# Linear attention and two MLPs on one core: the row of maxima of q, turned and merged earlier, its two halves sent by two DMA queues

## The chip, the core and the metric

The kernel runs on one core of a Trainium2 chip. Its engines are TensorE (PE, with its weight loads PEld), VectorE (DVE), ScalarE (ACT), GpSimd (POOL) and SyncE (SP), which here only issues DMAs. Each engine works through its own stream of instructions in order and waits on semaphores of the others. The metric is the device time of one execution in microseconds (us).

## What is computed

Four batches of eight heads, 576 rows of 64 numbers; `w_phi` has 128 features. The attention's output, one row of 512 per token, goes through two MLPs of 2304 tokens, which take most of the time and which the change doesn't touch.

```python
def phi(x):
    proj = np.einsum('bhsd,df->bhsf', x, w_phi)
    proj = proj - np.max(np.abs(proj), axis=-1, keepdims=True)
    return np.concatenate([np.exp(proj), np.exp(-proj)], axis=-1)
q_p, k_p = (phi(q), phi(k))
kv = np.einsum('bhsf,bhsd->bhfd', k_p, v)
z = np.sum(k_p, axis=2)
num = np.einsum('bhsf,bhfd->bhsd', q_p, kv)
den = np.einsum('bhsf,bhf->bhs', q_p, z)[..., None] + 1e-06
...
h = (x @ w1) * (x @ w2) @ w3
x = h @ w_out
h = np.maximum(x @ w_in, 0.0)
out = (h * h) @ w_out2
```

The maximum of `abs(proj)` is subtracted, for q, inside a PSUM tile in which a token is a column; so the maxima of q have to become a row.

## The kernel before

The attention runs over 16 units, t = 0 to 15: a unit is a pair of heads of one batch. Even units also do the tails (the last 64 rows of a head) of k for themselves and the next unit (`project_k2`, `peak_k2`, `less_k2`, `exp_k2`); odd units turn the tails of the two units that follow. In the traces a unit carries its batch and pair: unit 5 is 1_1, unit 6 is 1_2.

The order of all instructions on all engines is written by hand. `START` (line 29) is the order of the first unit and of what goes ahead of it. `SLOT` (line 35) is the order of every later unit: names of steps, run from left to right; in one slot, steps of unit t stand among steps of the unit behind it (its output) and the unit ahead (its transposes). Each engine gets its instructions in this order and never out of it.

The steps of unit t on which the change bears, with the engine and the tile that the profile names:

- `project_q` (line 369, PE): q times `w_phi`, into the one PSUM tile `pq`. Since there is only one, the next unit's `project_q` waits until `exp_q1` has read it. Its start is taken here as the start of a unit.
- `max_q` (line 384, DVE, `m<-pq` L387): maxima over 32 rows, into `m1`.
- `max_rows` (line 392, PE, `pm` L395): a 128x128 transpose of `m1` into PSUM.
- `max_parts` (line 397, DVE): two reductions of `pm`, once into `m` in full precision (L400), once into `mh[:, 0]`, rounded for the matmul (L402), and their difference into `mh[:, 1]` (L403). Then two DMAs (L406), both by SP, write the high and the low part into rows 0 and 1 of the one tile `mrow`.
- `minus_q` (line 410, PE, `pq<-mrow` L414): a matmul with a matrix of -1, which subtracts both rows from `pq`.
- `exp_q0`, `exp_q1` (line 418, ACT, `qp` L421).
- `peak_k0`, `less_k0`, `exp_k0` (lines 343 to 367): `kmax` on DVE (L348), the difference `kp<-pk,kmax` on DVE (L358), two exponentials on ACT (L365); then the same for half 1.
- `turn_k`, `high_k`, `low_k` (lines 296 to 308): four transposes `pkt` of the next unit's k (PE L288), their rounded part `kT` (ACT L291), the rest (DVE L294). `turn_q`, `high_q`, `low_q` are the same for q, `pqt` and `qT`.
- `out`, `keep` (lines 454 and 486): `po` of the unit behind (PE L459), copied to `nd` (ACT L488).
- `w-1`, `w0`, `w1`: a step of decoding a weight. Two ACT instructions of it (L137, L112) come ahead of `high_k`; four DVE instructions (L114, L117, L121, L124) come between `low_q` and the next unit's `max_q`.

Of the kernel before, what the change touches and what calls it, by code (L numbers as in the profile page):

```python
# [10 lines left out]
F32R = mybir.dt.float32r  # L11
I32 = mybir.dt.int32
AF = mybir.ActivationFunctionType
ALU = mybir.AluOpType
AX = mybir.AxisListType
# [17 lines left out]
warm8/0 values0/0 turn_q/0 minus_q/0 high_q/0 exp_q0/0 low_q/0 values1/0 exp_q1/0  # L33
""".split()
SLOT = """
load_kq product_b project_q keep_values project_k0 turn_w3b split_w3b x_load max_q project_k1 w1 w1 w0 early turn_k peak_k0
max_rows high_k less_k0 max_parts w-1 late store_x exp_k0 out x_split0 x_split1 x_split2 feature_sums peak_k1 less_k1
keep turn_q low_k turn_tails project_k2 product_a0 exp_k1 denominators spread peak_k2 less_k2 high_q minus_q exp_k2
keep_tails exp_q0 values0 gate last turn_w3 x_split3 low_q w0 w0 exp_q1 w0 values1 keep_rest low_tail reciprocals split_w3
product_a1 quotients keep_a load_v tail_values  # L40
# [4 lines left out]
def attention_then_mlps(ctx: ExitStack, tc: tile.TileContext, q, k, v, w_phi, w1, w2, w3, wo, wi2, wo2, out):  # L45
    nc = tc.nc
# [157 lines left out]
    with ExitStack() as actx:  # L204
        att = actx.enter_context(tc.tile_pool(name="att", bufs=2, side="right"))
# [52 lines left out]
        nb = S // 32  # L258
# [137 lines left out]

        def max_parts(z):
            pm = z["pm"][0:2 * nb]
            m = att.tile([2 * nb, 32], F32, tag="m", name=f"m_{z['nm']}")
            nc.vector.tensor_reduce(m, pm.rearrange("p (a r) -> p r a", a=4), AX.X, ALU.max)  # L400
            mh = att.tile([2 * nb, 2, 32], F32R, tag="mh", name=f"mh_{z['nm']}")
            nc.vector.tensor_reduce(mh[:, 0], pm.rearrange("p (a r) -> p r a", a=4), AX.X, ALU.max)  # L402
            nc.vector.tensor_tensor(out=mh[:, 1], in0=m, in1=mh[:, 0].bitcast(F32), op=ALU.subtract)  # L403
            z["mrow"] = mrow
            for s in range(2):
                nc.sync.dma_start(  # L406
                    z["mrow"][s:s + 1].bitcast(F32).rearrange("s (k r) -> s k r", r=32), mh[:, s].bitcast(F32)
                )

# [136 lines left out]
        w2h, w3s_at, queue, loaded, halves = {}, {}, [], [], []  # L546
# [55 lines left out]
        def even(f, *at):  # L602
# [3 lines left out]
        steps = {  # L606
            "keep_values": (-1, keep_values),
            "project_q": (0, project_q), "max_q": (0, max_q), "max_rows": (0, max_rows), "max_parts": (0, max_parts),
            "minus_q": (0, minus_q), "exp_q0": (0, lambda z: exp_q(z, 0)), "exp_q1": (0, lambda z: exp_q(z, 1)),
            "turn_k": (1, turn_k), "high_k": (1, high_k), "low_k": (1, low_k),  # L610
# [82 lines left out]
        with tc.manual_schedule(engines=mine):  # L693
            for entry in START:
                name, t = entry.split("/")
# [11 lines left out]
    late = ctx.enter_context(tc.tile_pool(name="late", bufs=2, side="right", reuse_waits="tile"))  # L707
# [4 lines left out]
    def lunit(dtype, shape, name, tag="w", bufs=RIGHT):  # L712
        return late.tile([P] + shape, dtype, tag=tag, bufs=bufs, name=name)
# [207 lines left out]
    with tc.manual_schedule(engines=mine):  # L921
# [5 lines left out]
        for s, (grp, at, k) in enumerate(steps):  # L927
# [26 lines left out]
            else:  # L954
# [8 lines left out]
                if k == HG - 1:  # L963
# [7 lines left out]
                    out=g[:, 1, 0:n], in0=g32[:, 0:n], in1=g[:, 0, 0:n].bitcast(F32), op=ALU.subtract  # L971
# [45 lines left out]
        for at, (b, n) in enumerate(mlp2):  # L1017
            cs, nt = nxt, n // P
            ops = None
            for j in range(NR):  # L1020
# [15 lines left out]
                if last_step:  # L1036
# [5 lines left out]
                    out=r32[:, 0:n], in0=ph[:, 0:n], scalar=0.0, in1=t[:, 0:n], op0=ALU.max, op1=ALU.mult  # L1042
                )
                if last_step:
                    col_split(x_in[nb_], nn, f"y{at}_{nb_}", [2])
                r = lunit(F32R, [2, 512], f"r_{b}_{j}", "g", 3)
# [3 lines left out]
                    out=r[:, 1, 0:n], in0=r32[:, 0:n], in1=r[:, 0, 0:n].bitcast(F32), op=ALU.subtract  # L1050
# [46 lines left out]
```

## Time and profile before

| | us |
|---|---|
| median of 3 runs | 943.4 (942.83 to 944.54) |
| the profiled execution | 942.8 |
| its span, first to last instruction | 941.0 |
| PE, share of the span | 98% |
| DVE, ACT, POOL, share of the span | 58%, 41%, 27% |

The page gives busy time by engine over the whole span, and the span has two parts. Up to some 195 us the attention runs, with all engines in use; after that the MLPs keep PE busy with matmuls that follow one another without a gap. An average over both says little of the attention. There, what counts is which wait ends last in each unit, and for that the trace is read unit by unit.

### The profile page before, as it was taken

Reading aid. Unit: us, or ns where it says so; the run is one execution under the profiler, and the core shown is the slowest. Engines: PE = TensorE matmul, PEld = TensorE weight load, DVE = VectorE, ACT = ScalarE, POOL = GpSimd, SP = SyncE. Lnnn points to the kernel's source line nnn. Section 1 sums busy time; section 2 is a strip of 40 time slices with the busy share of each in tenths; the row PEclk is TensorE's granted clock in tenths of the full one; section 3 lists DMA queues with packets and bytes.
Section 4 is the critical chain, followed back from the end, with each engine's and each line's share of the span. In section 5 each row is a group of like instructions: output and inputs, shape, how many; then the busy total and the mean of one; then the engine's idle time right before and its main releaser. Section 6 shows DMA issues by size and latency. Waiting matters only on the chain.

```text
span 941.0 us, 14857 instructions
## 1 busy us (share of the span) xinstructions
PE 921.3 (98%) x5915; PEld 762.2 (81%) x5915; DVE 545.7 (58%) x892; ACT 382.6 (41%) x689; POOL 249.6 (27%) x304
## 2 busy tenths in 40 slices
PE   8899999999999999999999999999999999999997
PEld 7677777778888988888988888888888888888896
DVE  5899888878656456666856688852224223322332
ACT  4777777653322334432333344342223223222322
POOL 1566556554121123333423145520000000000000
PEclk9999999999999999999999999999999999999999
DMA  6565556345241334254443433211002000100000
GB/s 164 125 161 150 145 153 182 89 149 160 87 135 54 127 111 157 68 202 157 166 152 117 147 114 111 90 39 51 1 1 90 1 1 0 68 1 1 23 24 23
DMA packets 81110, 89.24 MB, mean 95 GB/s; under 512 B 44624, under 2 KB 65680, under 8 KB 81040
## 3 DMA queue, kind: packets, MB, share of 16 engines
q1 hardware_dynamic: 79712, 87.72, 29.9%
q8 instruction: 47, 0.77, 0.4%
q10 hardware_dynamic: 1328, 0.56, 0.3%
q14 instruction: 23, 0.19, 0.1%
HBM read 69.76 MB, written 18.35 MB: 94 GB/s over the span
## 4 chain that ended last, share of the span: by engine, by line
PE 89%; DVE 4%; ACT 3%; DMA 2%; issue 1%; SPq 0%; ACTq 0%
PE ph L183 21%; PE op L905 21%; PE yp L887 11%; PE pb L183 11%; PE pa L183 10%; PE pf L844 5%; PE po L459 2%; PE pk L250 2%; PE pq L380 2%; ACT qp L421 2%; PE pkv L432 2%; DMA mrow<-mh 1%; PE pd L481 1%; DVE kmax L348 1%; DVE m L387 1%; ACT kp L365 1%
## 5 line engine op out<-in xcount | busy, mean ns | idle before, releaser
L905 PE MATMUL op<-w_w,r 128*128 128x512 f32 x864 | 209.6, 390 | 0.1
L905 PEld LDWEIGHTS op<-w_w,r 128*128 128x128 f32 x864 | 161.1, 188 | 33.4 <-ACT r L1047 0.5
L183 PE MATMUL ph<-y,w_w 128*128 128x512 f32 (+1 forms) x768 | 163.9, 362 | 0.0
L1041 DVE SCALAR_TENSOR_TENSOR r<-ph,t 128x512 f32<-128x512 f32 (+1 forms) x80 | 51.1, 639 | 187.8 <-ACT t L1039 187.8
L183 PEld LDWEIGHTS ph<-y,w_w 128*128 128x128 f32 x768 | 133.3, 189 | 23.8
L1039 ACT ACTIVATE t<-ph 128x512 f32<-128x512 f32 (+1 forms) x80 | 44.5, 556 | 215.5 <-PE ph L183 215.5
L887 PE MATMUL yp<-g,w3o 128*128 128x512 f32 (+1 forms) x480 | 106.1, 370 | 0.0
L129 POOL TENSOR_TENSOR dt_w<-dt_w,dy_w 128x512 f32<-128x512 f32 x48 | 62.9, 1310 | 126.2 <-DVE dy_w L124 126.1
L887 PEld LDWEIGHTS yp<-g,w3o 128*128 128x128 f32 x480 | 83.7, 189 | 14.8
L183 PE MATMUL pa<-c,w_w12a 128*128 128x512 f32 (+1 forms) x432 | 93.6, 366 | 0.0
L183 PE MATMUL pb<-c,w_w12b 128*128 128x512 f32 (+1 forms) x432 | 93.6, 366 | 0.0
L183 PEld LDWEIGHTS pa<-c,w_w12a 128*128 128x128 f32 x432 | 75.1, 189 | 13.2
L183 PEld LDWEIGHTS pb<-c,w_w12b 128*128 128x128 f32 x432 | 75.2, 189 | 13.1
L1049 DVE TENSOR_TENSOR r<-r,r 128x512 fp32r<-128x512 f32 (+1 forms) x80 | 51.0, 638 | 41.2 <-ACT r L1047 37.5
L966 DVE TENSOR_TENSOR g<-pb,a 128x512 f32<-128x512 f32 (+1 forms) x39 | 24.8, 636 | 84.6 <-PE pb L183 80.0
L139 POOL TENSOR_TENSOR w_w<-dt_w,w_w 128x512 fp32r<-128x512 f32 x32 | 48.8, 1527 | 84.2 <-ACT w_w L137 84.2
L1047 ACT ACTIVATE r<-r 128x512 fp32r<-128x512 f32 (+1 forms) x80 | 47.2, 590 | 55.9 <-DVE r L1041 55.9
L506 POOL TENSOR_SCALAR rc<-dc 32x9 f32<-32x9 f32 x128 | 45.5, 356 | 57.8 <-DVE dc L496 50.7
L968 ACT ACTIVATE g<-g 128x512 fp32r<-128x512 f32 (+1 forms) x39 | 23.0, 589 | 91.7 <-DVE g L966 91.7
L958 ACT COPY a<-pa 128x512 f32<-128x512 f32 (+1 forms) x39 | 21.2, 543 | 81.2 <-PE pa L183 81.2
L365 ACT ACTIVATE kp<-kp 128x512 f32<-128x512 f32 (+1 forms) x80 | 46.9, 588 | 17.3 <-DVE kp L358 15.1
L121 DVE TENSOR_SCALAR dy_w<-dt_w 128x512 int32<-128x512 int32 x48 | 50.9, 1061 | 0.7
(135 smaller groups left out, 1282.0 us busy)
## 6 DMA issues: line engine op xcount, KB each, us to landing
x<-x_hbm SPq DMA_DIRECT2D x16, 512.0 KB
raw_w<-in_moe_w_dram SPq DMA_DIRECT2D x16, 512.0 KB
raw_w<-in_moe_w_in_dram SPq DMA_DIRECT2D x16, 512.0 KB
raw_w<-in_moe_w_out_dram SPq DMA_DIRECT2D x16, 512.0 KB
qm<-in_q_dram SPq DMA_DIRECT2D x32, 128.0 KB
km<-in_k_dram SPq DMA_DIRECT2D x16, 256.0 KB
vs<-in_v_dram SPq DMA_DIRECT2D x32, 128.0 KB
raw_wo<-in_moe_w_out_dram SPq DMA_DIRECT2D x8, 512.0 KB
```

Source lines behind the costliest of these rows:

```text
L121: nc.vector.tensor_scalar(out=e, in0=t, scalar1=-(1 << 23), scalar2=None, op0=ALU.bitwise_and)
L129: nc.gpsimd.tensor_tensor(out=w, in0=t.bitcast(F32), in1=e.bitcast(F32), op=ALU.add)
L139: nc.gpsimd.tensor_tensor(out=dst[:, 1], in0=w[0], in1=dst[:, 0].bitcast(F32), op=ALU.subtract)
L183: nc.tensor.matmul(ps[:, 0:n], a, c, start=kk + i == 0, stop=kk == KD - 1 and i == 2)
L365: nc.scalar.activation(z["kp", j][:, :, s, :], z["kp", j][:, :, 1, :], AF.Exp, scale=1.0 - 2.0 * s)
L506: nc.gpsimd.tensor_scalar(out=z["rc2"][i * 32:(i + 1) * 32, s, :], in0=z["dc"][at * 32:(at + 1) * 32, :], scalar1=1e-6, scalar2=None, op0= ...
L844: nc.tensor.matmul(pf, a, c, start=g + j + n == 0, stop=g == 1 and j == 3 and n == 2)
L887: nc.tensor.matmul(blk.yp[i][:, 0:blk.n], a, d, start=c % HG + s == 0, stop=c % HG == HG - 1 and s == 2)
L905: nc.tensor.matmul(ops[i], a, d, start=j + s == 0, stop=j == NR - 1 and s == 2)
L1041: nc.vector.scalar_tensor_tensor(out=r32[:, 0:n], in0=ph[:, 0:n], scalar=0.0, in1=t[:, 0:n], op0=ALU.max, op1=ALU.mult)
L1047: nc.scalar.activation(r[:, 0, 0:n], r32[:, 0:n], AF.Copy)
L1049: nc.vector.tensor_tensor(out=r[:, 1, 0:n], in0=r32[:, 0:n], in1=r[:, 0, 0:n].bitcast(F32), op=ALU.subtract)
```

## The change

In `SLOT`, `max_rows` goes ahead of `turn_k`, and `max_parts` ahead of `less_k0`. `START` is as it was. In `max_parts` the rounded reduction into `mh[:, 0]` now comes ahead of the one into `m`, and the DMA of the high row is issued by ACT (`nc.scalar`), that of the low row by SP. Sixteen DMA issues move from SP to ACT; no instruction is added or taken away.

```diff
-load_kq product_b project_q ... w1 w1 w0 early turn_k peak_k0
-max_rows high_k less_k0 max_parts w-1 late store_x exp_k0 out ...
+load_kq product_b project_q ... w1 w1 w0 early max_rows turn_k
+peak_k0 high_k max_parts less_k0 w-1 late store_x exp_k0 out ...
...
         def max_parts(z):
             pm = z["pm"][0:2 * nb]
+            view = pm.rearrange("p (a r) -> p r a", a=4)
+            mh = att.tile([2 * nb, 2, 32], F32R, tag="mh", name=f"mh_{z['nm']}")
+            nc.vector.tensor_reduce(mh[:, 0], view, AX.X, ALU.max)
             m = att.tile([2 * nb, 32], F32, tag="m", name=f"m_{z['nm']}")
-            nc.vector.tensor_reduce(m, pm.rearrange("p (a r) -> p r a", a=4), AX.X, ALU.max)
-            mh = att.tile([2 * nb, 2, 32], F32R, tag="mh", name=f"mh_{z['nm']}")
-            nc.vector.tensor_reduce(mh[:, 0], pm.rearrange("p (a r) -> p r a", a=4), AX.X, ALU.max)
+            nc.vector.tensor_reduce(m, view, AX.X, ALU.max)
             nc.vector.tensor_tensor(out=mh[:, 1], in0=m, in1=mh[:, 0].bitcast(F32), op=ALU.subtract)
             z["mrow"] = mrow
-            for s in range(2):
-                nc.sync.dma_start(
+            for s, queue in enumerate((nc.scalar, nc.sync)):
+                queue.dma_start(
                     z["mrow"][s:s + 1].bitcast(F32).rearrange("s (k r) -> s k r", r=32), mh[:, s].bitcast(F32)
                 )
```

On PE in unit 6, before (`pk` is the projection of k, `pkt` the turned k of unit 7, `pm` the turned maxima, `po` the output of unit 5):

```order
L250 MATMUL pk_1_2_0_1268<-wbd_132,kT_1_2_1113 128x256 x6
L250 MATMUL pk_1_2_1_1276<-wbd_132,kT_1_2_1113 128x256 x6
L288 MATMUL pkt_1_3_1288<-ident_73,km_1_3_1068 128x128 x4
L395 MATMUL pm_1_2_1295<-ident_73,m1_0_97 128x128
L459 MATMUL po_1_1_1312<-qp_1_1_1186,kv_1_1_1264 64x512 x4
```

The same place after the change:

```order
L250 MATMUL pk_1_2_0_1268<-wbd_132,kT_1_2_1113 128x256 x6
L250 MATMUL pk_1_2_1_1276<-wbd_132,kT_1_2_1113 128x256 x6
L395 MATMUL pm_1_2_1288<-ident_73,m1_0_97 128x128
L288 MATMUL pkt_1_3_1290<-ident_73,km_1_3_1068 128x128 x4
L460 MATMUL po_1_1_1312<-qp_1_1_1186,kv_1_1_1264 64x512 x4
```

`pm`, which needs `max_q`, now stands directly behind `pk`, with the four transposes of k behind it instead of ahead of it.

On DVE in unit 5, before:

```order
L387 TENSOR_REDUCE m1_1_98<-pq_1_1_1070 128x36
L348 TENSOR_REDUCE kmax_1_1_0_1109<-pk_1_1_0_1084 128x4
L358 TENSOR_TENSOR kp_1_1_0_1115<-pk_1_1_0_1084,kmax_1_1_0_1109 128x4x128
L400 TENSOR_REDUCE m_1_1_1117<-pm_1_1_1111 36x32
L402 TENSOR_REDUCE mh_1_1_1119<-pm_1_1_1111 36x32
L403 TENSOR_TENSOR mh_1_1_1119<-m_1_1_1117,mh_1_1_1119 36x32
L348 TENSOR_REDUCE kmax_1_1_1_1151<-pk_1_1_1_1092 128x4
```

After:

```order
L387 TENSOR_REDUCE m1_1_98<-pq_1_1_1070 128x36
L348 TENSOR_REDUCE kmax_1_1_0_1111<-pk_1_1_0_1084 128x4
L401 TENSOR_REDUCE mh_1_1_1115<-pm_1_1_1104 36x32
L403 TENSOR_REDUCE m_1_1_1117<-pm_1_1_1104 36x32
L404 TENSOR_TENSOR mh_1_1_1115<-m_1_1_1117,mh_1_1_1115 36x32
L358 TENSOR_TENSOR kp_1_1_0_1122<-pk_1_1_0_1084,kmax_1_1_0_1111 128x4x128
L348 TENSOR_REDUCE kmax_1_1_1_1151<-pk_1_1_1_1092 128x4
```

The three instructions of `max_parts` now stand ahead of the difference `kp`, for which ACT's exponentials wait.

On ACT in the same unit, before:

```order
L291 ACTIVATE kT_1_2_1113<-pkt_1_2_1104 128x512
L365 ACTIVATE kp_1_1_0_1115<-kp_1_1_0_1115 128x4x128 x2
L488 COPY nd_1_0_1155<-po_1_0_1129 128x512
L365 ACTIVATE kp_1_1_1_1153<-kp_1_1_1_1153 128x4x128 x2
L291 ACTIVATE qT_1_2_1179<-pqt_1_2_1157 128x512
L291 ACTIVATE tT_1_2_1184<-ptt_1_2_1163 128x256
L421 ACTIVATE qp_1_1_1186<-pq_1_1_1070 128x1152 x2
```

After:

```order
L291 ACTIVATE kT_1_2_1113<-pkt_1_2_1106 128x512
L407 DMA mrow_99<-mh_1_1_1115 1x36x32
L365 ACTIVATE kp_1_1_0_1122<-kp_1_1_0_1122 128x4x128 x2
L489 COPY nd_1_0_1155<-po_1_0_1129 128x512
L365 ACTIVATE kp_1_1_1_1153<-kp_1_1_1_1153 128x4x128 x2
L291 ACTIVATE qT_1_2_1179<-pqt_1_2_1157 128x512
L291 ACTIVATE tT_1_2_1184<-ptt_1_2_1163 128x256
L422 ACTIVATE qp_1_1_1186<-pq_1_1_1070 128x1152 x2
```

The issue of the high row stands between `kT` and the first exponentials of k, and everything that ACT does for the unit is queued behind it.

## Rows read from the trace of the kernel before

**Rows 1.** Windows, core 0: length, busy PE PEld DVE ACT POOL, clock, DMA share, GB/s.

```profile
55.77:67.27 11.50, 10.82 (x151) 8.33 (x149) 10.79 (x22) 8.76 (x17) 7.09 (x13) 1.00 0.53 145
67.27:77.76 10.49, 10.49 (x148) 8.13 (x149) 8.89 (x17) 8.50 (x16) 6.82 (x12) 1.00 0.59 145
89.25:100.81 11.56, 10.61 (x149) 8.13 (x147) 9.92 (x20) 8.63 (x16) 7.79 (x13) 1.00 0.60 162
122.80:134.72 11.92, 10.73 (x152) 8.32 (x150) 11.19 (x23) 8.92 (x16) 7.52 (x14) 1.00 0.58 153
156.75:168.33 11.58, 10.60 (x147) 8.13 (x147) 9.94 (x20) 8.52 (x16) 7.83 (x13) 1.00 0.78 231
205.00:941.00 736.00, 730.23 (x3470) 613.53 (x3469) 376.36 (x574) 237.25 (x429) 139.21 (x104) 1.00 0.24 80
```

**Rows 2.** Waits of PE, 20 to 181 us: total us, times, longest.

```profile
PE pq L414 <- DMA mrow<-mh: 5.8, 6, 1.3
```

**Rows 3.** Timeline, unit 7: start, us, engine, line, operation [idle before, releaser].

```profile
93.64 1.69 SPq L406 DMA_DIRECT2D mrow<-mh  x2
...
97.66 0.76 PE L414 MATMUL pq<-mrow,minus 128*128 128x512 f32 x3 [0.95 <-DMA mrow<-mh]
```

**Rows 4.** Chain that ended last, unit 7: start, us, what.

```profile
94.55 2.97 DMA mrow<-mh
```

**Rows 5.** Timeline of DVE, units 5 and 6.

```profile
70.55 0.69 DVE L358 TENSOR_TENSOR kp<-pk,kmax 128x512 f32<-128x512 f32 x1
71.16 0.27 DVE L400 TENSOR_REDUCE m<-pm 36x32 f32<-36x128 f32 x1
...
75.17 0.69 DVE L294 TENSOR_TENSOR qT<-pqt,qT 128x512 fp32r<-128x512 f32 x1 [0.70 <-ACT qT L291]
...
79.36 1.34 DVE L387 TRANSPOSE_TENSOR_REDUCE m<-pq 128x36 f32<-128x1152 f32 x1
```

**Rows 6.** Timeline of ACT, unit 5.

```profile
70.60 0.60 ACT L291 ACTIVATE kT<-pkt 128x512 fp32r<-128x512 f32 x1 [0.81 <-PE pkt L288]
71.28 1.29 ACT L365 ACTIVATE kp<-kp 128x512 f32<-128x512 f32 x2
72.59 0.59 ACT L488 COPY nd<-po 128x512 f32<-128x512 f32 x1
73.21 1.30 ACT L365 ACTIVATE kp<-kp 128x512 f32<-128x512 f32 x2
74.54 0.60 ACT L291 ACTIVATE qT<-pqt 128x512 fp32r<-128x512 f32 x1
75.03 0.38 ACT L291 ACTIVATE tT<-ptt 128x256 fp32r<-128x256 f32 x1
75.40 2.15 ACT L421 ACTIVATE qp<-pq 128x1152 f32<-128x1152 f32 x2
```

**Rows 7.** Timeline of PE, unit 6.

```profile
80.45 0.60 PE L288 MATMUL pkt<-ident,km 128*128 128x128 f32 x4
80.89 0.27 PE L395 MATMUL pm<-ident,m 128*128 128x128 f32 x1
```

**Rows 8.** Timeline of DVE and PEld, unit 1.

```profile
23.48 1.38 DVE L387 TRANSPOSE_TENSOR_REDUCE m<-pq 128x36 f32<-128x1152 f32 x1
...
24.91 0.14 PEld L395 LDWEIGHTS pm<-ident,m 128*128 128x128 f32 x1 [1.15 <-DVE m L387]
```

**Rows 9.** Lines L406 and L242: queue, operation, count, ns min/median/max, first and last start.

```profile
L406 SPq DMA_DIRECT2D mrow<-mh x32: 737/791/921, 14.4 to 185.1; - x32
...
L242 ACTq DMA_DIRECT2D qtl<-in_q_dram x2: 655/666/676, 1.4 to 2.1; - x2
```

**Rows 10.** Timeline of ACT, units 0 and 15.

```profile
14.04 1.29 ACT L365 ACTIVATE kp<-kp 128x512 f32<-128x512 f32 x2 [3.91 <-DVE kp L358]
...
185.04 1.66 ACT L148 ACTIVATE x<-x 128x512 fp32r<-128x512 f32 x3
```

**Rows 11.** Timeline of PE at the end of unit 15.

```profile
193.92 2.35 PE L183 MATMUL pb<-x,w_w12b 128*128 128x512 f32 x9 [0.27 <-ACT a L635]
```

More of the change, by code (lines that the diff above doesn't have):

```diff
@@ L35 @@
 SLOT = """
-load_kq product_b project_q keep_values project_k0 turn_w3b split_w3b x_load max_q project_k1 w1 w1 w0 early turn_k peak_k0
-max_rows high_k less_k0 max_parts w-1 late store_x exp_k0 out x_split0 x_split1 x_split2 feature_sums peak_k1 less_k1
+load_kq product_b project_q keep_values project_k0 turn_w3b split_w3b x_load max_q project_k1 w1 w1 w0 early max_rows turn_k
+peak_k0 high_k max_parts less_k0 w-1 late store_x exp_k0 out x_split0 x_split1 x_split2 feature_sums peak_k1 less_k1
 keep turn_q low_k turn_tails project_k2 product_a0 exp_k1 denominators spread peak_k2 less_k2 high_q minus_q exp_k2
```

## The prediction

> **What bounds the kernel now.** First the windows. Behind 205 us PE is busy for 730.23 of 736.00 us [rows 1]; nothing of the change lies there, so those microseconds stay, and whatever the attention ahead of them gains or loses goes into the end one for one. In the attention I take each unit from the start of its `project_q` to the next one's. An odd unit that waits for nothing is unit 5: 10.49 us, all of it PE busy. An even unit is unit 4: 11.50 us, though PE is busy for 10.82 of them. Units 7 and 13 are odd and take 11.56 and 11.58, unit 10 is even and takes 11.92 [rows 1]. So three units stand out, by 1.07, 1.09 and 0.42 us.
>
> Next, who PE waits for. The row of the DMA of the maxima says 5.8 us in six waits [rows 2]. That is not what can be won: it counts the waits of units 2 and 6 too (they end no later than unit 4 does), since in even units a second chain sets the end, `turn_q`, `project_k2`, the exponentials of that tail, then `exp_q`. It starts from PE, and no maximum of q is in it. What the row is worth is read from the units' lengths: 1.07 + 1.09 + 0.42 = 2.58 us, and part of unit 1's wait.
>
> The chain in unit 7: SP issues the high row at 93.64 and the low one some 0.9 us behind it, the two taking 1.69; PE starts `minus_q` at 97.66 after 0.95 us of waiting [rows 3]; the chain gives 2.97 us from the second issue to the landing [rows 4].
>
> **The change, part by part.** *The rows of maxima land earlier.* The low row needs no longer stand behind the issue of the high one (0.79 us, the median of L406 [rows 9]), and `max_parts` begins 0.61 us earlier, by the step that it overtakes (70.55 to 71.16 [rows 5]). Together 1.4 us against a wait of 0.95, so that the wait goes in units 7 and 13, and in 10 nearly so: −2.58 us.
>
> The Trainium skill's page "DMA: Bandwidth & Descriptors", section "Issuing engines are not separate DMA queues", speaks against half of this: DMAs of different engines share the same DMA engines, and issuing from several saves only the sequencer's time. By it the second queue gives one issue and no shorter flight; the sum takes no more than that, so it stays −2.58.
>
> *`max_rows` ahead of `turn_k`, on PE.* The transposes of k used to run while `max_q` ended. In unit 6 they begin at 80.45, and `pm` at 80.89, when `max_q` (79.36, 1.34 long) had just ended at 80.70 [rows 5, 7]. Now `pm` stands where `pkt` stood and PE waits for `max_q` with nothing ahead. How fast PE goes on then, unit 1 shows: `max_q` ends at 24.86, the weight load of `pm` starts at 24.91 [rows 8], 0.05 later. So with DVE as it was: 80.70 + 0.05 − 80.45 = 0.30 us of PE idle in an even unit.
>
> In odd units `max_q` begins right behind `project_q`, since the even unit ahead left DVE idle; there the order costs some 0.1 us, PE's hand-over alone.
>
> *`max_parts` ahead of `less_k0`, on DVE and ACT.* `less_k0` starts 0.61 us later, and the first exponentials of k with it: from 71.28 to 71.89 in unit 5 [rows 6]. Behind them on ACT stand `nd`, the second exponentials, `qT`, `tT` and `exp_q`. In unit 5 this row has no slack: each starts as the one ahead ends. But three of them (72.59, 73.21, 74.54) started 0.02 to 0.03 us after that end, because each was waiting for another engine as well; an instruction that waits for nobody starts before the end of the one ahead, as `tT` does at 75.03, with `qT` running from 74.54 for 0.60 [rows 6], thus 0.11 ahead. Three times 0.13 gives back 0.4: `qT` and `exp_q` move by some 0.2. `exp_q` would then start at 75.6, last 2.15 and let PE go on at 77.8; PE itself, 0.1 late, gets there at 77.9 instead of 77.76. I book 0.12 for an odd unit, six times (3 to 13): +0.7.
>
> *The two together.* `low_q` on DVE waits for `qT` (75.17, after 0.70 of idle time), and from there DVE runs without a gap into the next unit's `max_q` at 79.36 [rows 5]. So `max_q` of the even unit comes 0.2 later while the unit begins 0.12 later. Its end is then 80.92, `pm` at 80.97, PE's place for it 80.57 by matmuls and some 0.1 sooner by the weight load that goes ahead: 0.40 to 0.50 of PE idle, and I take 0.47. It was nothing, as `pkt` covered it. It is on the path of an even unit, because the chain that sets its end begins with PE's `turn_q` behind it. Units 2, 8 and 14 stood well with DVE before only because the long units 1, 7 and 13 let it catch up; once those are short, they are like 4 and 6. Seven even units (2 to 14): +3.3. Bounds: 0.30 from above if ACT's delay doesn't reach DVE, and 0.55 if it does in full (below).
>
> *The issue on ACT.* No row shows ACT issuing this DMA. Its nearest price is SP's for the same one, 737 to 921 ns, and ACT's own for the tails of q, 655 to 676 [rows 9]; I take 0.79. In slots the issue can begin when the high part is there, about 70.87 in unit 5, and ends at 71.66, ahead of 71.89 when the exponentials may start: free, as long as it can run beside `kT` (70.60 to some 71.4, `pkt` being later by `pm`). If ACT has to end `kT` first, the exponentials start at 72.25 instead, 0.37 later. I take free, and the other as a rival.
>
> By the Trainium skill, page "Perfetto Trace Analysis", sections "DVE / Act Engine Instruction" and "DMA Instruction — HWDGE", a compute instruction is handed to a queue ahead of its engine and the sequencer goes on, while a DMA holds the sequencer from its wait to the end of its issue. This supports "beside `kT`", and warns of the rest: all of ACT behind it is held. No row here shows either.
>
> *Both ends.* In `START` the issue stands ahead of unit 0's first exponentials, which now start at 14.04 [rows 10]. The high part is ready at about 14.2, the issue ends at 15.0: 1.0 late, of which 0.25 is made up as above, so unit 1 starts 0.75 late. It gets this back: its wait for the row, the longest of all, goes, and then PE's own work ends the unit: −0.2 for units 0 and 1 together. Unit 15 is followed by no `turn_q`; ACT's exponentials are followed by the splits of x at 185.04, and ACT still ends the wait ahead of `pb` at 193.92 [rows 10, 11]. The 0.61 goes through to there, and PE's 0.1: +0.7.
>
> *Nothing:* the swap of the two reductions (the high part 0.2 sooner, the group as long as before), and SP, which issues the raw weights one issue sooner and is waited for nowhere else.
>
> **Sum:** −2.6 + 0.7 + 3.3 − 0.2 + 0.7 = +1.9, with roundings +2.0 us. The profiled execution has 942.8 (a span of 941.0 and 1.8 around it), so 944.8; the median of the three runs lies 0.6 above it, at 943.4, and against that I forecast **945.4**.
>
> **The rivals.**
>
> 1. *Faster: DVE is in time.* If `max_q` ends no later than PE reaches `pm`, then the wait for the DMA goes and nothing takes its place. The place is `max_q` of even units; for it, the stretch of DVE from `low_q` to `max_q` (4.19 us [rows 5]) must end 0.3 us sooner than it did. For: only seven units need it, and PE, DVE and ACT settle into a rhythm that I read from two units. Against: no row shortens that stretch, and four even units had no idle time ahead of `max_q` already. Price: −2.58 and some 0.9 of unit 1's wait, the longest with 1.3 [rows 2], so 943.4 − 3.5 = 939.9. It decides from 0.2 us per even unit downwards.
> 2. *No change: ACT takes up its delay.* The even units then lose 0.30, the odd ones 0.1, the ends nothing: 2.1 + 0.6 − 2.58 − 0.2 = −0.1, and up to 0.8 less if unit 1 wins its whole wait: 942.5 to 943.4.
> 3. *Slower by more: the issue holds ACT behind `kT`.* Exponentials 0.37 later still: `exp_q` at 76.0, an odd unit longer by 0.43, an even one by 0.52: 6 × 0.43 + 7 × 0.52 − 2.58 + 0.3 + 0.75 = +4.7, so 948.1.
> 4. *It doesn't do what it says:* the row still lands late, by something that follows the queues and not the issue. Then the 2.58 stays: 948.0. Against it: even at 2.97 us of flight [rows 4], the low row, issued 0.61 sooner than the high one was and one small step behind it, at about 93.3, is there at 96.3, before PE has ended `turn_q` and the tails in unit 7.
>
> **How the numbers follow.** The forecast (944.3 to 946.8) gets 0.47; the rivals 0.14, 0.22, 0.12 and 0.05. About 0.2% (1.9 us) is what a measurement of this kernel can tell from no change. Two thirds of the forecast's case lie above 945.3, and rivals 3 and 4 all: slower 0.48. The rest of it and rival 2: same 0.38. Rival 1: faster 0.14. The range leaves out rival 1 and the far ends, and runs from 942.0 to 948.6.
>
> **What the profile after would show.** Right: PE's waits for `mrow` nearly gone; a new wait of PE's `pm` for DVE's L387, about 0.4 to 0.5 us in each of the seven even units; even units near 12.0, odd ones near 10.6, 7 and 13 among them; the first exponentials of k 0.6 later against `project_q`; ACT's issue ahead of them and ended in time. Wrong: odd units near 10.9 (rival 3); even ones below 11.8 (rival 2) or at 11.5 (rival 1); waits for `mrow` of 1 us in units that are not slowed (rival 4).

## The result, and the profile after

| | us |
|---|---|
| kernel before, median of 14 runs beside it | 942.6 (940.4 to 947.8) |
| changed kernel, median of 14 runs | 948.0 (946.7 to 952.3) |
| ratio | 1.0055 (95%: 1.0040 to 1.0071) |
| the same, measured once more | 948.6 against 943.5, ratio 1.0051 (1.0037 to 1.0066) |

The change costs 5.2 us, with 3.8 to 6.7 as the interval. The forecast was 945.4, some 2 us above before, with a range of 942.0 to 948.6. The direction and most of the mechanism came as forecast, and 948.0 lies in the range; the size of the loss is more than twice the 2 us.

The windows of the changed kernel by units (columns as in [rows 1]): units 5, 6, 7, 10 and 13.

```profile
70.72:81.26 10.54, 10.52 (x147) 8.12 (x147) 8.78 (x17) 8.03 (x16) 6.76 (x12) 1.00 0.64 165
81.26:93.38 12.12, 10.86 (x150) 8.33 (x150) 11.46 (x22) 8.67 (x18) 6.61 (x12) 1.00 0.56 144
93.38:103.92 10.54, 10.51 (x148) 8.11 (x149) 8.79 (x17) 8.02 (x16) 6.76 (x12) 1.00 0.65 172
126.57:138.68 12.11, 10.85 (x149) 8.33 (x150) 11.46 (x22) 8.67 (x18) 6.61 (x12) 1.00 0.56 143
161.33:175.60 14.27, 12.26 (x147) 9.72 (x148) 10.67 (x20) 8.20 (x16) 9.56 (x15) 0.88 0.66 204
```

Against [rows 1], odd units went from 10.49 to 10.54, even ones from 11.50 to 12.12. Units 7 and 10, which stood out before, are now like their neighbours. Unit 13 is not: 14.27. Two of PE's waits from 20 to 181 us, in the form of [rows 2], say the same:

```profile
PE pm L395 <- DVE m L387: 2.5, 7, 0.5
PE pq L415 <- DMA mrow<-mh: 2.0, 1, 2.0
```

Of the 5.8 us for rows of maxima 2.0 are left, all in unit 13; a wait of `pm` for `max_q` has come, seven times and up to 0.5.

**Where the time went.** This profiled execution (952.3 us) is the longest of the 14, mostly by unit 13. So the account is made with the profile of the repetition (948.9 us; its unit 13 takes 11.38), against that of before (942.8 us). Windows of before: units 0, 1, 2 to 13, 14, from there to the first `pb`, and the rest.

```profile
9.64:20.70 11.06, 8.99 (x118) 7.86 (x117) 7.20 (x14) 6.79 (x12) 0.00 (x0) 1.00 0.51 132
20.70:33.77 13.07, 10.83 (x147) 8.19 (x147) 11.35 (x22) 8.50 (x16) 5.64 (x11) 1.00 0.57 148
33.77:168.33 134.56, 127.69 (x1772) 98.63 (x1770) 118.62 (x223) 104.41 (x186) 83.57 (x145) 1.00 0.59 159
168.33:179.84 11.51, 10.57 (x152) 8.26 (x150) 9.93 (x19) 8.98 (x17) 6.08 (x13) 1.00 0.30 83
179.84:193.92 14.08, 13.69 (x153) 9.88 (x153) 9.65 (x18) 9.29 (x19) 4.71 (x11) 1.00 0.45 147
193.92:941.00 747.08, 741.31 (x3544) 621.62 (x3544) 384.66 (x590) 241.86 (x439) 145.65 (x111) 1.00 0.24 80
```

The same stretches of the changed kernel, repeated:

```profile
9.37:23.31 13.94, 11.45 (x117) 10.24 (x117) 7.32 (x14) 6.58 (x12) 0.00 (x0) 1.00 0.60 160
23.31:36.44 13.13, 10.84 (x148) 8.15 (x148) 11.13 (x19) 8.52 (x16) 5.06 (x10) 1.00 0.33 88
36.44:172.87 136.43, 128.54 (x1772) 98.72 (x1770) 122.06 (x224) 100.24 (x186) 80.39 (x145) 1.00 0.57 158
172.87:184.46 11.59, 10.66 (x151) 8.27 (x150) 10.54 (x21) 8.64 (x17) 6.58 (x12) 1.00 0.28 73
184.46:199.02 14.56, 13.99 (x153) 9.80 (x153) 9.56 (x18) 9.29 (x19) 4.69 (x11) 1.00 0.45 146
199.02:947.10 748.08, 741.37 (x3544) 621.81 (x3544) 383.51 (x590) 241.68 (x439) 145.52 (x111) 1.00 0.24 80
```

| stretch | booked | measured |
|---|---|---|
| ahead of unit 0 | 0 | -0.27 |
| units 0 and 1 | -0.2 | +2.88 and +0.06 |
| units 2 to 13 | -2.6 + 0.7 + 2.8 = +0.9 | +1.87 |
| unit 14 | +0.5 | +0.08 |
| unit 15 up to `pb` | +0.7 | +0.48 |
| behind `pb` | 0 | +1.00 |

Two of these are not all the change's. Behind `pb` nothing was changed, and the 14 profiles of this study scatter there from 746.4 to 748.1, without regard to the kernel. In unit 0 the first twelve matmuls of `pk` took 2.93 us in this execution and 1.68 in that of before. They follow one another by 0.21 us in the one and by 0.12 in the other, which is the pace of the lower and of the higher of TensorE's two clock levels (1.2 and 2.4 GHz). In each of the 14 traces the record of the granted clock begins where the pace goes up: at 9.4 to 11.3 us in the quick kind (before: 10.5), at 14.6 to 15.7 in the slow one (here: 15.7). Ahead of that place the 1.00 in the windows stands on no record. The slow kind came up in kernels with ACT's issue in unit 0 (three of five profiles) and without it (three of nine). Ahead of `pk` all the kernels have the same instructions, and from 5.0 to 9.5 us PE was busy for 4.3 to 4.5 us in the slow kind and 3.9 to 4.5 in the quick one; why the clock rose late in some executions, no run tells. Compared like with like, unit 0 took 12.25 and 12.36 with ACT's issue against 11.06 before, where the clock rose 0.8 to 1.0 us into the unit, and 13.94 against 12.72 (g3), where it rose 6.3 us into it: the issue costs about 1.2 us, and the rest of the +2.88 is the clock's.

### The profile page after: what moved, and what is told of

The parts are those of the page before. It is cut to its first block, busy times and chain, and to the rows that moved or that the text cites. A ratio compares the mean times of both kernels' runs of the same rounds, so it can differ in the third digit from the quotient of the medians.

```text
span 949.7 us, 14862 instructions
## 1 busy us (share of the span) xinstructions
PE 927.2 (98%) x5915; PEld 766.8 (81%) x5915; DVE 548.2 (58%) x892; ACT 377.6 (40%) x689; POOL 246.1 (26%) x304
## 4 chain that ended last, share of the span: by engine, by line
PE 84%; DVE 7%; ACT 5%; DMA 2%; issue 1%; SPq 0%; ACTq 0%
PE ph L183 21%; PE op L906 21%; PE yp L888 10%; PE pb L183 10%; PE pa L183 10%; PE pf L845 5%; ACT kp L365 3%; ACT qp L422 2%; DVE m L387 2%; PE po L460 1%; PE pq L380 1%; DVE kmax L348 1%; PE pd L482 1%; DMA mrow<-mh 1%; PE pk L250 1%
## 5 line engine op out<-in xcount | busy, mean ns | idle before, releaser
L129 POOL TENSOR_TENSOR dt_w<-dt_w,dy_w 128x512 f32<-128x512 f32 x48 | 62.8, 1308 | 127.4 <-DVE dy_w L124 127.3
L139 POOL TENSOR_TENSOR w_w<-dt_w,w_w 128x512 fp32r<-128x512 f32 x32 | 48.8, 1526 | 84.2 <-ACT w_w L137 84.2
L507 POOL TENSOR_SCALAR rc<-dc 32x9 f32<-32x9 f32 x128 | 42.2, 330 | 60.3 <-DVE dc L497 53.2
L121 DVE TENSOR_SCALAR dy_w<-dt_w 128x512 int32<-128x512 int32 x48 | 50.9, 1061 | 0.7
```

The source lines that it names most:

```text
L121: nc.vector.tensor_scalar(out=e, in0=t, scalar1=-(1 << 23), scalar2=None, op0=ALU.bitwise_and)
L129: nc.gpsimd.tensor_tensor(out=w, in0=t.bitcast(F32), in1=e.bitcast(F32), op=ALU.add)
L139: nc.gpsimd.tensor_tensor(out=dst[:, 1], in0=w[0], in1=dst[:, 0].bitcast(F32), op=ALU.subtract)
```

## The experiments

Theories: **A**, the prediction's: the new order is the loss, PE's `pm` waiting for `max_q`, with a delay of ACT that is mostly made up; a mis-sized unit 0 explains the rest. **B**: the issue on ACT is the loss. **C**: an accident of one profile. **D**, formed on the first four runs: an instruction of `max_parts` collides with one of POOL, that is, it is held until POOL's has ended. Columns: ratio to the kernel before with its interval; the usual even and odd unit, and their sum, where no row was late.

| kernel | median | ratio | even + odd |
|---|---|---|---|
| before | 942.6 to 943.5 | 1 | 11.50 + 10.49 = 22.0 |
| e1 changed, repeated | 948.6 | 1.0051 (1.0037 to 1.0066) | 12.10 + 10.55 = 22.65 |
| e2 `max_rows` ahead, alone | 945.8 | 1.0023 (1.0011 to 1.0036) | 11.92 + 10.48 = 22.40 |
| e3 `max_parts` ahead, alone | 944.4 | 1.0012 (1.0001 to 1.0023) | 11.83 + 10.82 = 22.65 |
| e4 second queue, alone | 947.2 | 1.0042 (1.0025 to 1.0059) | 11.78 + 10.82 = 22.60 |
| f1 changed, low part by way of PSUM | 947.0 | 1.0044 (1.0030 to 1.0058) | 12.13 + 10.60 = 22.73 |
| f2 e3, low part by way of PSUM | 945.0 | 1.0021 (1.0011 to 1.0030) | 11.67 + 10.90 = 22.57 |
| f3 changed, all rows by SP | 946.4 | 1.0039 (1.0027 to 1.0052) | 12.11 + 10.54 = 22.65 |
| f4 changed, unit 0's row by SP | 946.9 | 1.0048 (1.0033 to 1.0063) | 12.11 + 10.55 = 22.66 |
| g1 changed, POOL writes zeros | 946.8 | 1.0043 (1.0031 to 1.0055) | 11.99 + 10.45 = 22.44 |
| g2 step split in two | 942.3 | 0.9997 (0.9986 to 1.0008) | 11.68 + 10.37 = 22.05 |
| g3 before, low row by POOL | 952.2 | 1.0097 (1.0084 to 1.0110) | no unit without a late row to go by |
| h1 g2, high row by ACT | 942.0 | 0.9989 (0.9973 to 1.0004) | 11.67 + 10.37 = 22.04 |

**e1, the changed kernel again.**

> The changed kernel once more, beside its parts on one chip. It was 5.2 us above the kernel before. Theory A (the order is the loss: `pm` ahead of `pkt` lets PE wait for `max_q` in even units, and the deltas of units 0 and 1 were mis-sized): even units at 12.1 us, odd ones at 10.54 as in its first profile, unit 2 starting some 2 us later than before, whatever the clock does. Theory B (the second queue is the loss, ACT issuing a DMA): the same lengths, so this run alone does not tell; it gives the reference for the others. Theory C (the first profile caught a lower clock and a late DMA in units 0, 1 and 13): unit 0 at some 11.5 to 12.0 instead of 13.65, unit 13 at 10.54 instead of 14.27. In all cases +4 to +6 us against before.

C is out as the cause of the loss: 948.6, and again 12.10 and 10.55. It holds for unit 13 (11.38 now); unit 0 had the low clock again, 13.94 this time.

**e2, `max_rows` alone.**

```diff
-... w1 w1 w0 early turn_k peak_k0
-max_rows high_k less_k0 max_parts w-1 ...
+... w1 w1 w0 early max_rows turn_k peak_k0
+high_k less_k0 max_parts w-1 ...
```

> One part alone: `max_rows` ahead of `turn_k`; `max_parts` stays behind `less_k0`, both rows by SP. Theory A: PE waits for `max_q` some 0.3 us in the even units, whose DVE is late (4, 6, 10, 12), nothing is won at the landing of the rows, since DVE takes up `pm` no sooner: units 7 and 13 stay at 11.5; +1.2 to +2.0 us against before. Theory B: no ACT issue, so no loss: within 0.5 us of before.

Units 4 and 5 of this kernel:

```profile
57.46:69.38 11.92, 10.79 (x151) 8.26 (x149) 10.91 (x22) 8.80 (x17) 7.14 (x13) 1.00 0.53 144
69.38:79.86 10.48, 10.48 (x148) 8.15 (x149) 8.80 (x17) 8.25 (x16) 6.72 (x12) 1.00 0.55 143
```

Against [rows 1] the even unit is 0.42 longer, the odd one unchanged. This part of A stands: a transpose put ahead of work that had covered the end of `max_q` costs 0.4 us in even units, with no new queue. The whole, 2.2 us by the ratio, is a little over the 1.2 to 2.0 expected.

**e3, `max_parts` alone.**

```diff
-max_rows high_k less_k0 max_parts w-1 ...
+max_rows high_k max_parts less_k0 w-1 ...
```

> One part alone: `max_parts` ahead of `less_k0`; `max_rows` stays behind `turn_k`, both rows by SP. Theory A: the rows land some 0.6 us sooner in units 1, 7 and 13, where PE waited for 0.95 to 1.3, and the odd units lose 0.05 each: -1 us, between -1.8 and +0.5. Theory B: the same. A rival to both, that the step put ahead of the exponentials of k is what makes the even units long (ACT late, `qT` late, DVE late): even units at 11.7 or more, and +1 to +2 us.

A expected -1 us and lost; the rival of this run, the step ahead of the exponentials, came: even units 11.83, and odd ones 10.82. Alone the step costs as much per pair as the whole new order. Its size is the surprise: it holds `less_k0` up by more than its own 0.61. The place is easiest to see in the changed kernel, where both steps are moved; unit 8:

```profile
107.51 1.28 POOL L139 TENSOR_TENSOR w_wo<-dt_wo,w_wo 128x512 fp32r<-128x512 f32 x1
...
108.05 0.73 ACTq L407 DMA_DIRECT2D mrow<-mh  x1
108.10 0.73 DVE L404 TENSOR_TENSOR mh<-m,mh 36x32 fp32r<-36x32 f32 x1
108.76 0.67 DVE L358 TENSOR_TENSOR kp<-pk,kmax 128x512 f32<-128x512 f32 x1
109.47 1.29 ACT L365 ACTIVATE kp<-kp 128x512 f32<-128x512 f32 x2 [0.91 <-DVE kp L358]
```

L404, the difference of 36x32 elements, ends at 108.83, just behind POOL's L139 (108.79). In odd units it takes 0.43 and ends with L139 too, in unit 1 of the repetition 1.19. Before it took 0.18, starting behind L139's end: by 0.8 us in unit 8 (105.20 against 104.39), by 0.3 in the usual odd unit and by only 0.03 in the usual even one. Moving the step forward moved it into POOL's instruction. That is theory D. Before the change there was one such place, in unit 1:

```profile
25.73 1.28 POOL L139 TENSOR_TENSOR w_wo<-dt_wo,w_wo 128x512 fp32r<-128x512 f32 x1 [0.74 <-ACT w_wo L137]
...
26.58 0.46 DVE L403 TENSOR_TENSOR mh<-m,mh 36x32 fp32r<-36x32 f32 x1
```

27.04 against 27.01: the row was in the trace from which the prediction was made.

**e4, the second queue alone.** The new `max_parts` (as in the change's diff), with the order of before.

> One part alone: the high row by ACT, with the rounded reduction first; the order of the steps as before. Here the high part is there only behind `less_k0`, so that ACT's exponentials, for which `less_k0` has already released ACT, stand behind an issue that waits for a later step. Theory A: exponentials of k some 0.9 to 1.0 us later against `project_q`, odd units 0.3 to 0.4 longer, START 1 us: +2 to +4, and this loss is not in the changed kernel outside of unit 0. Theory B: the issue itself is the loss: +4 to +6, as the changed kernel, with even units near 12.1.

As A expected, odd units 10.82 and +3.7 us by the medians. Here `less_k0` comes first, so ACT could have begun, but the issue stands ahead. In unit 8 (`less_k0` runs from 107.58):

```profile
108.50 0.73 ACTq L407 DMA_DIRECT2D mrow<-mh  x1
...
109.27 1.30 ACT L365 ACTIVATE kp<-kp 128x512 f32<-128x512 f32 x2 [1.24 <-DVE mh L404]
```

The exponentials begin 0.04 us behind the end of the issue (109.23). ACT's queue is in order for DMAs too. In the changed kernel the same issue ends at 108.78, ahead of the exponentials at 109.47, and costs nothing there.

**f1 and f2, the difference without two operands in SBUF** (the edit is shortened).

```diff
-            m = att.tile([2 * nb, 32], F32, ...)
-            nc.vector.tensor_reduce(m, view, AX.X, ALU.max)
-            nc.vector.tensor_tensor(out=mh[:, 1], in0=m, in1=mh[:, 0], op=ALU.subtract)
+            m = att.tile([2 * nb, 4, 32], F32, ...)
+            nc.vector.tensor_tensor(out=m, in0=pm (4 x 32), in1=mh[:, 0] (broadcast), op=ALU.subtract)
+            nc.vector.tensor_reduce(mh[:, 1], m ("p a r -> p r a"), AX.X, ALU.max)
```

> The changed kernel, but the low part of the maxima is made without an instruction of DVE that reads two operands from SBUF: instead of a maximum into `m` and `m - mh`, the difference of `pm` (PSUM) and `mh` is taken first, and its maximum then. As many instructions, as many waits of others, the same order. Theory D, formed on the last four runs: in the changed kernel the difference at L404 takes 0.73 us in even units and 0.43 in odd ones instead of 0.18, and ends each time with POOL's L139, whose 1.28 us it now meets; `less_k0`, ACT's exponentials and the rest of the loop stand behind it. By D the two instructions take some 0.3 each in every unit, a pair of units falls from 22.65 to 22.1 to 22.45 (what is left is PE's wait for `max_q`, which came to 0.43 in the run with `max_rows` alone), unit 1 loses its 1.1 us: 2 to 4 us less than the changed kernel, +1 to +3 against before. Theory A (only PE's wait and the first unit): no lock to remove, pairs stay at 22.65, same time as the changed kernel or 0.5 us more for the larger instructions.

> `max_parts` ahead of `less_k0` alone, both rows by SP, `max_rows` behind `turn_k` as before, and the low part without two operands in SBUF. With the lock this order gave +1.1 us against before and pairs of units of 22.65. Theory D: pairs at 22.0 to 22.1 and the rows 0.5 to 0.6 us sooner in units 1, 7 and 13: -1.0 to -2.5 us against before, so 941 to 942.5. Theory that the step ahead of the exponentials costs by itself (0.6 of ACT's loop per unit): pairs still at 22.4 or more, +0.5 to +1 against before.

Both missed: pairs of 22.73 and 22.57. The runs do not speak against D, they are a poor test of it. No instruction waited for POOL any more, but the three now depend on each other and on larger tiles: 0.30, 0.31 and 0.38, so 0.99 from the first one's start to the last one's end (f1, unit 10: 128.77 to 129.76), where the colliding form took 1.22 in an even and 0.92 in an odd unit. One price took the place of another. They show something else: in f1 `less_k0` starts 0.22 sooner in even units than in the changed kernel and 0.06 later in odd ones (4.62 and 4.08 us into the unit against 4.84 and 4.02), and the pair gets 0.08 longer. So it is the odd unit's delay that counts there.

**f3 and f4, where ACT's issue counts.** f3 sends all rows by SP, in the new order; f4 those of unit 0 alone.

```diff
 f3
-            for s, queue in enumerate((nc.scalar, nc.sync)):
+            for s, queue in enumerate((nc.sync, nc.sync)):
 f4
+            for s, queue in enumerate((nc.scalar if z["before"] else nc.sync, nc.sync)):
```

> The changed kernel with both rows sent by SP: the whole new order, and no issue on ACT. Theory D: the pairs stay at 22.65 (the lock is there as before), units 0 and 1 win the 2.1 us by which ACT's issue of 1.36 us held the first exponentials, some 1.1 us of it on the path; rows land 0.7 to 0.8 us later than in the changed kernel, up to 0.3 us of waiting in units 7 and 13: 0.5 to 1.5 less than the changed kernel, +3.5 to +4.5 against before. Theory B (the second queue is the loss): pairs at 22.0 to 22.1, within 1 us of before.

> The changed kernel, but the high row of unit 0 goes by SP (the other fifteen by ACT). In unit 0 of the changed kernel the first exponentials start 2.8 us behind the start of `less_k0`, against 0.7 us where SP sends the row. By this reading the exponentials start 0.7 us behind it again, unit 0 is 1.0 to 1.2 us shorter at the same pace of PE, and the whole 0.8 to 1.3 us shorter than the changed kernel. If the first unit's delay is made up in unit 1, as the prediction had it (-0.2 for both): no difference to the changed kernel.

In f3 the pairs are 22.65 with no issue on ACT at all: B is out for the slots. For unit 0, first the changed kernel, then f4:

```profile
14.04 0.69 DVE L358 TENSOR_TENSOR kp<-pk,kmax 128x512 f32<-128x512 f32 x1
15.47 1.36 ACTq L407 DMA_DIRECT2D mrow<-mh  x1
...
16.87 1.29 ACT L365 ACTIVATE kp<-kp 128x512 f32<-128x512 f32 x2 [6.86 <-DVE kmax L348]
```

```profile
13.57 0.69 DVE L358 TENSOR_TENSOR kp<-pk,kmax 128x512 f32<-128x512 f32 x1
14.30 1.29 ACT L365 ACTIVATE kp<-kp 128x512 f32<-128x512 f32 x2 [4.12 <-DVE kp L358]
```

From the start of `less_k0` to the exponentials 2.83 us in the one, 0.73 in the other, and unit 0 takes 11.27 in f4. The changed kernel's profile had the low clock in unit 0; at the high one it is 2.31 (g1: 15.38 behind 13.07). By the ratios f3 lies 1.1 to 1.5 us under the changed kernel and f4 0.3 to 0.7, where 0.5 to 1.5 and 0.8 to 1.3 were expected, but the intervals of the ratios overlap; that ACT's issue holds the exponentials is shown, its 1.2 us in the whole time rests on the traces.

**g1, POOL writes zeros at L139** (the low parts of the decoded weights are left out).

```diff
-        nc.gpsimd.tensor_tensor(out=dst[:, 1], in0=w[0], in1=dst[:, 0].bitcast(F32), op=ALU.subtract)
+        nc.gpsimd.memset(dst[:, 1].bitcast(F32), 0.0)
```

> The changed kernel; at L139 POOL writes zeros into the low part of each decoded weight instead of reading two operands and writing their difference (the low parts are left out of the computation). Everything else, the two instructions of DVE among it, is as in the changed kernel. Theory D (the difference of the maxima at L404 waits until POOL's L139 has ended): L404 takes 0.18 us in every unit instead of 0.73 and 0.43, `less_k0` starts 0.55 and 0.25 sooner, and pairs of units fall from 22.65 to 22.0 to 22.45, the upper end being what `max_rows` ahead of `turn_k` alone gave; unit 1 loses some 0.9: 2 to 4.5 us less than the changed kernel. If L404 is long for another reason (the high part not yet written, a busy PSUM): it stays at 0.4 to 0.7, and the time at the changed kernel's.

Unit 8, and the windows of units 9 and 10:

```profile
104.39 0.53 POOL L139 MEMSET w_wo<- 128x512 f32 x1
...
105.00 0.18 DVE L404 TENSOR_TENSOR mh<-m,mh 36x32 fp32r<-36x32 f32 x1
105.10 0.67 DVE L358 TENSOR_TENSOR kp<-pk,kmax 128x512 f32<-128x512 f32 x1
```

```profile
112.92:123.37 10.45, 10.45 (x147) 8.12 (x147) 8.66 (x17) 8.12 (x16) 5.91 (x12) 1.00 0.58 167
123.37:135.35 11.98, 11.03 (x150) 8.31 (x148) 10.89 (x22) 8.66 (x17) 6.45 (x13) 1.00 0.56 143
```

L404 takes 0.18 in all 16 units, so D is shown: it was L139 that held it. Whether POOL's reading did it or its mere running is not: the new L139 takes 0.53 instead of 1.28 and has ended (104.92) when L404 starts (105.00), here and in every unit. Pairs fall to 22.44, the figure of `max_rows` alone, and unit 1 to 11.94. So of the 0.65 per pair 0.44 stay with PE's wait for `max_q` and 0.21 are the collision. With no collision the odd unit loses nothing. The medians fell by 1.2 to 1.8 us, the ratios by 0.8 to 1.1, under the 2 to 4.5 expected, and the intervals of the ratios overlap; the traces' units carry the point.

**g2, the step split.**

```diff
-max_rows high_k less_k0 max_parts w-1 ...
+max_rows high_k max_parts less_k0 low_parts w-1 ...
```

`max_parts` keeps both reductions and the high row's DMA; `low_parts` has the difference and the low row's DMA; both rows by SP.

> The two reductions and the issue of the high row ahead of `less_k0`; the difference and the issue of the low row behind it; both by SP; `max_rows` behind `turn_k` as before. Theory D: the difference starts when it started in the kernel before, behind POOL's L139, and takes 0.18; `less_k0` starts some 0.5 later than before instead of 0.86 to 1.16; the loop of DVE and ACT then has some 21.7 to 22.0 per pair, no more than PE's: pairs at 22.0 to 22.2, and the low row issued some 0.7 us sooner in units 1, 7 and 13: -0.5 to -2.5 us against before. If any delay of `less_k0` goes through: 0.5 twice per pair, less 0.4 of slack: pairs at 22.5, +0.5 to +2.

Unit 9:

```profile
114.35 1.26 POOL L139 TENSOR_TENSOR w_w12a<-dt_w12a,w_w12a 128x512 fp32r<-128x512 f32 x1
...
115.31 1.67 SPq L413 DMA_DIRECT2D mrow<-mh  x2
115.41 0.67 DVE L358 TENSOR_TENSOR kp<-pk,kmax 128x512 f32<-128x512 f32 x1
116.01 0.17 DVE L409 TENSOR_TENSOR mh<-m,mh 36x32 fp32r<-36x32 f32 x1
```

The difference stands behind L139 again in odd units; in even ones it still meets its end and takes 0.23. `less_k0` starts 4.08 us into an even unit and 3.85 into an odd one; before it was 3.55 and 3.28, in the changed kernel 4.84 and 4.02. So the split delays it by 0.53 and 0.57, and the pair keeps 22.05: a delay of that size is taken up, nearly as the prediction had it for 0.61, and e3's, of 1.29 and 1.02 with `max_rows` in the same place, is not. The time is that of the kernel before, within 0.15%; the 0.5 to 2.5 us that earlier rows were expected to give did not come.

**g3, the low row by POOL, in the kernel before.**

```diff
-            for s in range(2):
-                nc.sync.dma_start(
+            for s, queue in enumerate((nc.sync, nc.gpsimd)):
+                queue.dma_start(
```

> The kernel before with one word changed: the low row is issued by POOL instead of SP, no order changed. What the second queue is worth by itself, with nothing put ahead of anything: the low row is issued some 0.8 us sooner, so that PE's waits in units 1, 7 and 13 (0.95 to 1.3) fall to 0.2 to 0.5: -1.5 to -2.5 us against before, pairs at 22.0. Against it: POOL has its decoding and its reciprocals behind the issue, and no run shows how long an issue on POOL takes; at over 2 us its L139 or L506 end late, and the row lands later than by SP: 0 to +2.

Slower by 9 us, where 1.5 to 2.5 less was expected; in the profile units 1 to 13 hold 6.9 of it, and unit 0 with its low clock 1.7. The issue in unit 7, the row's way in the chain of that stretch, and PE's waits from 20 to 181 us:

```profile
99.84 0.80 SPq L406 DMA_DIRECT2D mrow<-mh  x1
100.56 0.58 POOL L406 DMA_DIRECT2D mrow<-mh  x1 [1.05 <-issue]
```

```profile
100.56 3.92 DMA mrow<-mh
```

```profile
PE pq L414 <- DMA mrow<-mh: 10.1, 9, 1.9
```

POOL issues 0.72 us behind SP's start, where SP itself did so 0.91 behind [rows 3, 4], so 0.19 are saved. The row then needs 3.92 us against 2.97 [rows 4], in unit 13 3.82 against 2.99, in unit 10 1.95 against 1.94; over the 16 units it is 1.8 to 3.9, with a median of 2.9. Why it is longer where it is, no run shows. Here the second queue saved less in issue than its row lost in flight.

**h1, the split, with the high row by ACT in units 1 to 15.**

```diff
+            queue = nc.scalar if s == 0 and z["before"] else nc.sync
```

> The split order of the last run (both reductions ahead of `less_k0`, the difference behind it, `max_rows` behind `turn_k`), and the high row issued by ACT in units 1 to 15, by SP in unit 0. In the split run the pairs took 22.05 where no row was late, PE waited 4.2 us for rows in six waits, and SP issued the high row at the end of a train of other issues. With ACT: the high part is there 0.3 us behind the first reduction's start, the issue takes 0.73 and ends at about 116.0 in the times of the split run's unit 9, just ahead of the exponentials at 116.12: free by this reading, pairs stay at 22.0 to 22.1, the waits for rows fall to 2 us or less: -0.5 to -2.5 us against before, and a version that beats both kernels. If ACT's issue is not free there (its sequencer is held until the issue has ended, and the exponentials start late): exponentials 0.3 or more later, pairs at 22.4 or more, +1 to +3 against before.

Unit 9, and PE's waits for rows from 20 to 181 us:

```profile
116.80 0.72 ACTq L414 DMA_DIRECT2D mrow<-mh  x1
116.89 0.67 DVE L358 TENSOR_TENSOR kp<-pk,kmax 128x512 f32<-128x512 f32 x1
...
117.60 0.63 ACT L365 ACTIVATE kp<-kp 128x512 f32<-128x512 f32 x1 [0.62 <-DVE kp L358]
```

```profile
PE pq L422 <- DMA mrow<-mh: 2.7, 4, 1.4
```

The issue ends at 117.52 under `less_k0`, and ACT waits for `less_k0`, not for the queue: free. Pairs 22.04, units 2 to 13 in 132.95 us against 134.56 before. It is 6 us under the changed kernel; against the kernel before the ratio reaches from -0.27% to +0.04%, so that a gain is likely but not shown.

## Why the prediction came out as it did

- **What bounds the kernel:** right. Behind the first `pb` the kernel takes 747 to 748 us as before, and what the units lost came out at the end.
- **The rows land earlier (-2.58):** right in units 7 and 10 (10.54 and 12.11, as their neighbours). Wrong in unit 13. Its low row was issued 4.12 us into the unit instead of 5.31, but its flight grew. In the chain of that stretch, and on PE:

```profile
165.45 5.30 DMA mrow<-mh
```

```profile
170.88 0.76 PE L415 MATMUL pq<-mrow,minus 128*128 128x512 f32 x3 [2.01 <-DMA mrow<-mh]
```

  2.99 before, 3.96 in the repetition, 5.30 here. The step that failed took the flight as fixed. The DMA engines move x and a weight in this unit (204 to 245 GB/s in the three profiles, where units 2 to 12 have 121 to 190), but so they did before; what made the flight longer is not shown. In the repetition some 1.7 of the 2.58 came. In the first profile, PE's clock fell besides: 0.88 granted in that unit, behind a wait of 2.0 us.
- **`max_rows` ahead of `turn_k` (0.30, with the delay 0.47 per even unit):** right in kind and place, and near in size. Alone it took 0.42 (e2, against the 0.30), with the delay and no collision 0.49 (g1, against the 0.47).
- **`max_parts` ahead of `less_k0` (0.61 on DVE, 0.12 in odd units):** the step mis-sized. The 0.61 holds only where nothing collides; with L139 it was 0.25 to 0.55 later still. The prediction looked at ACT's and DVE's rows and left out POOL's. Which part of the delay counts, the changed kernel's chain that ended last tells, in units 8 (even) and 9:

```profile
105.84 1.28 DVE m L387
...
107.16 0.33 PE pm L395
...
112.61 0.43 DVE kp L358
...
113.07 0.43 ACT kp L365
...
120.77 0.63 ACT kp L365
```

  In the even unit it goes from `max_q` by `pm` and PE to the difference of the tail (112.61) and its exponentials; the unit's own `less_k0` (108.76) is not in it, so the 0.55 lost there cost nothing. In the odd unit it goes by the first exponentials (120.77), `qT` and the decoding on DVE into the next `max_q`; those exponentials waited for `less_k0`, which ended 0.04 ahead of them, while the issue had ended 0.41 ahead. There the exponentials come 0.72 later than before, and `qT` 0.32: ACT makes up 0.4, as the prediction had it. The odd unit's delay thus reaches `max_q` and adds to PE's wait, and the 0.25 of the collision in odd units makes about the 0.21 per pair. In e3, with `pm` behind `pkt`, the even unit's `less_k0` is in the chain, and its 22.65 come about another way. In all 0.65 per pair, against 0.59 booked; six pairs give 3.9.
- **The issue on ACT:** free in the slots, as taken (f3, h1); rival 3 is out. It takes 0.73 there, 0.79 was booked.
- **Units 0 and 1 (-0.2):** the term that failed most. Unit 0's issue took 1.36, not 0.79, and held the exponentials 1.6 us at the high clock (2.1 at the low one) instead of 1.0; the unit became 1.2 longer. Unit 1 was to give it back and did not (13.07 before, 12.80 and 13.13 after): in the repetition PE waits 1.35 for `max_q` there, instead of 0.91, and 0.95 of its wait for the row are left, and L404 takes 1.1 to 1.2 us beside L139, where it had taken 0.46 before.
- **The end (+0.7, and 0.5 for unit 14):** +0.48 and +0.08. Unit 14 was booked with units 7 and 13 short; unit 13 was late again, and DVE caught up in it, as it had before.

Put together by these figures, the change costs 3.9 - 0.3 (unit 2 was short in the repetition) - 1.7 + 1.2 + 0.1 + 0.1 + 0.5 = +3.8, the lower end of the measured interval. Some 1.4 us of the measured difference stay open; unit 13's flight and unit 0's pace of matmuls, which vary from one execution to the next, could hold it, but no run tells. That the range held is in part luck: its upper end takes in rivals 3 and 4, whose prices of 948.1 and 948.0 the measured time meets, and neither of them came (odd units took 10.54, and no unit but 13 waited for its row in the first profile).

## What to carry to other kernels

A step that is moved has to be laid beside every other engine's rows at its new time, those included that it neither feeds nor waits for: here an instruction of POOL, 1.28 us long, had ended 0.03 to 0.8 us ahead of the difference's old place. Earlier is not better as a whole: what has a reader that waits (the two reductions, the first row) can go ahead, what has none yet (the difference) can stay behind, and that split kept the units' pace where moving the whole step lost 0.65 per pair (e3). A DMA issue put on a compute engine is free only where that engine is waiting for something that ends later than the issue; look at the first unit by itself.

## What the runs showed of the hardware

- **A DVE instruction with two operands in SBUF waits for a POOL `TENSOR_TENSOR` that began ahead of it.** The 36x32 difference took 0.18 alone, 0.43, 0.73 and 1.19 beside POOL's L139, ending 0.03 to 0.04 us behind it. Of the decoding in the changed kernel, the nine instructions at L117 and L124 that started while L129 or L139 ran took 1.66 to 1.67 instead of 0.69. `less_k0`, with one operand in PSUM, ran beside L139 for its usual 0.69 (unit 1 before, and 0.67 in g2). The Trainium skill, page "SBUF — State Buffer", section "Who interferes with whom", states the rule: a DVE instruction with two inputs in SBUF contends with a GpSimd instruction that reads SBUF, not with one that only writes it, and one with at most one such input does not contend, outside the 2-port perf modes. The traces agree for the difference and for `less_k0`; no run here has a POOL instruction that only writes beside the difference. L121, with one input in SBUF, is held as well (1.51 to 1.53 us beside L139 later than 200 us, 0.43 alone); whether it runs in such a mode, no row shows.
- **The first row that ACT issues takes 1.36 us, the others 0.73**: in unit 0 of the changed kernel, in unit 1 where unit 0's row goes by SP (f4, h1: 1.36 and 1.35). Why, no run shows.
- **A row of 4.5 KB takes 1.8 to 5.3 us from issue to landing** where the traces show it, by the stretch and the execution; by POOL's queue 1.8 to 3.9.
